# Chunked attention and a bilinear feed-forward: the output product of blocks 2 to 8 as seven half-block products in fp16

## The chip, the cores and the metric

The kernel runs on one NeuronCore of a Trainium2 chip. The metric is the device time of one execution in microseconds. A bank is a 128x512 fp32 tile of PSUM, the memory in which this kernel's matmul results lie. The engines are named as the profile names them: PE is TensorE (PEld its weight loads), DVE is VectorE, ACT is ScalarE, POOL is GpSimd, SP issues DMA.

## The reference, cut to what matters

```python
# attention in chunks of 64 tokens: q, k, v are (8, 8, 576, 64), about 0.1 in size
scores = scale * np.matmul(q_c, k_c.transpose(0, 1, 2, 4, 3))
attn = np.exp(scores - max);  attn = attn / (sum(attn) + 1e-09)
x = np.matmul(attn, v_c)                 # as 4608 tokens x 512
# feed-forward: w_a, w_b are 512 x 1536, w_out is 1536 x 512
a = x @ w_a
b = x @ w_b
return (a * b) @ w_out
```

## The kernel before

The 4608 tokens are nine blocks of 512 (K = 0 to 8), each of two attention units of 256 tokens. The program order of each engine is the order of the source. Blocks 0 and 1 compute a and b directly. From block 2 on a and b come from seven half-block products in place of eight (a Strassen scheme: sums of quarters of x, named s1 to s4, meet differences of quarters of the weights, named t1 to t4). A block has six groups i = 0 to 5 of 256 columns of w_a and w_b. Between the products of a group lie two slots with parts of the previous block's output product (`chunk`), and pieces of the attention of the next block (`attend`).

The parts that the change and the argument touch:

```python
def cast_ab(i):                          # weights fp32 -> fp16, on GpSimd
    for n in ("wb", "wa"):
        w_ab[n, i] = wpool.tile([128, NKT, WCOL], FP16, name=f"{n}{i}")
        nc.gpsimd.tensor_copy(out=w_ab[n, i], in_=staged.pop((n, i)))

class Group:                             # seven products, f16, 256 moving columns each
    def p1(self):
        self.A = bank(psum)
        self.product(self.A, self.b11, self.x11, True)
        self.B = bank(psum_b)
        nc.scalar.copy(out=self.B, in_=self.A)
    # ... p6, p2, p5: a product into B or A, then a ScalarE copy u, b or v to SBUF
    def p7(self):
        self.C = bank(psum_c)
        self.product(self.C, self.t3, self.s3, True)
    def add7(self):                      # VectorE: c = C + v, then C = C + u
        ...
    def p4(self):                        # adds to C, so it waits for C + u
        self.product(self.C, self.t4, self.x22)
        self.multiply(self.C, self.c, 256)

def out_part(K, tg, part):               # a third of a direct output product
    for ft in range(4 * part, 4 * part + 4):
        nc.tensor.matmul(out_ps[K, tg], ab_tiles[K][:, ft, tg * 128:tg * 128 + 128],
                         w_out[ft], ...)  # 512 moving columns, bf16

# ... attention pieces of the next block: unit U in groups 0 to 2, unit U + 1 in groups 2 to 4
((4, 1), values_x, U + 1),               # second slot of group 4: attention products,
                                         # then all four sums of x (combine_x) on VectorE
# ...
for K in range(2, NBLK):
    for i in range(NWP):
        now.p1(); last.add7(); chunk(); last.p3(); attend(K, i, 0)
        now.p6(); now.p2(); last.p4(); chunk(); attend(K, i, 1)
        now.p5(); now.p7(); last = now
```

The softmax here doesn't subtract the row's maximum and nothing guards it: scores larger than these inputs give would overflow.

Of the kernel before, what the change touches and what calls it, by code (L numbers as in the profile page):

```python
# [10 lines left out]
PE_UNITS = 6  # L11


@with_exitstack
def kernel(
# [36 lines left out]
    st_pool = ctx.enter_context(tc.tile_pool(name="st", bufs=9))  # L52
# [3 lines left out]
    x_pool = ctx.enter_context(tc.tile_pool(name="xp", bufs=3))  # L56
    s_pool = ctx.enter_context(tc.tile_pool(name="sp", bufs=2))
    ab_pool = ctx.enter_context(tc.tile_pool(name="ab", bufs=2))
    c_pool = ctx.enter_context(tc.tile_pool(name="csb", bufs=1))
    o_pool = ctx.enter_context(tc.tile_pool(name="osb", bufs=6))  # L60
    psum = ctx.enter_context(tc.tile_pool(name="psum", bufs=4, space=PSUM))
    psum_b = ctx.enter_context(tc.tile_pool(name="psumb", bufs=2, space=PSUM))
    psum_c = ctx.enter_context(tc.tile_pool(name="psumc", bufs=2, space=PSUM))
# [10 lines left out]
    spread = [psum, psum_b, psum, psum_c]  # L74

    def bank(pool=None):
        if pool is None:
            pool = spread[0]
            spread.append(spread.pop(0))
        n = {id(psum): "ps", id(psum_b): "pb", id(psum_c): "pc"}[id(pool)]  # L80
        return pool.tile([128, 512], FP32, name=n)
# [20 lines left out]
    def cast_ab(i):  # L102
        for n in ("wb", "wa"):
            w_ab[n, i] = wpool.tile([128, NKT, WCOL], FP16, name=f"{n}{i}")
            nc.gpsimd.tensor_copy(out=w_ab[n, i], in_=staged.pop((n, i)))
# [3 lines left out]
    def combine_w(i, part):  # L109
        wb, wa = w_ab["wb", i], w_ab["wa", i]  # L110
        b11, b12, b21, b22 = wb[:, 0:2], wa[:, 0:2], wb[:, 2:4], wa[:, 2:4]
        if i not in w_t:
            w_t[i] = [wpool.tile([128, 2, WCOL], FP16, name=f"t{j}_{i}") for j in range(1, 5)]
        t1, t2, t3, t4 = w_t[i]
        o, x0, x1, op = (
            (t1, b12, b11, SUB), (t3, b22, b12, SUB), (t2, t3, b11, ADD), (t4, b21, t2, SUB)
        )[part]
        nc.vector.tensor_tensor(out=o, in0=x0, in1=x1, op=op)
# [7 lines left out]

    def cast_wo(i):
        t = wpool.tile([128, 2, DM], BF16, name=f"wo{i}")
        nc.gpsimd.tensor_copy(out=t, in_=staged.pop(("wo", i)))
        for f in range(2):  # L130
            w_out[2 * i + f] = t[:, f, :]


# [37 lines left out]
    def cast(U, names="qkv"):  # L171
        for n in names if U < NU else "":
            raw[n, U] = raw_pool.tile(
                [128, 2, H, D], BF16, name=f"{n}_raw", bufs=4 if n == "v" else 3
            )
            eng = nc.vector if U == 0 and n != "v" else nc.gpsimd
            eng.tensor_copy(out=raw[n, U], in_=staged.pop((n, U)))  # L177
# [54 lines left out]
    def sums(U, halves=None):  # L232
        E = E_of[U]
        sm = [bank() for _ in range(2)]
        for cl in range(2):
            for j in range(2):
                nc.tensor.matmul(  # L237
                    sm[cl][j * 64:j * 64 + 64, :],
                    ones[cl * 64:cl * 64 + 64, :],
                    E[cl * 64:cl * 64 + 64, j].rearrange("p m g s -> p (m g s)"),  # L240
                    start=True,
                    stop=True,
                )
        ln_of[U] = sm_pool.tile([128, 2, NKT, 128], FP32, name="ln")
        rs_of[U] = ln_of[U]
        for cl in range(2):
            nc.scalar.activation(  # L247
                out=ln_of[U][:, cl].rearrange("p m n -> p (m n)"), in_=sm[cl], func=AF.Ln
            )
            if halves:  # L250
                inverse(U, cl)
# [60 lines left out]
    def ab_tile(K):  # L312
        if K not in ab_tiles:
            ab_tiles[K] = ab_pool.tile([128, NFT, BLK], BF16, name="ab_sb")
        return ab_tiles[K]

    def ab_step(K, ft, c0=0, c1=BLK):
        xT = x_tiles[K]
        dst = ab_tile(K)
        i, o = divmod(ft * 128, WCOL)  # L320
        ps = {}
        whole = c1 - c0 == BLK
        for n, pool in (
            ("wb", psum_b if whole else psum),
            ("wa", (psum_c, psum)[ft % 2]),
        ):
            ps[n] = bank(pool)[:, :c1 - c0]
            for kt in range(NKT):
                nc.tensor.matmul(  # L329
                    ps[n],  # L330
                    w_ab[n, i][:, kt, o:o + 128],
                    xT[:, kt, c0:c1],
                    start=(kt == 0),
                    stop=(kt == NKT - 1),
                )
        b_sb = c_pool.tile([128, BLK], FP32, name=("b_sb", "u_sb", "v_sb", "c_sb")[ft % 4])
        nc.scalar.copy(out=b_sb[:, :c1 - c0], in_=ps["wb"])
        nc.vector.tensor_tensor(
            out=dst[:, ft, c0:c1], in0=ps["wa"], in1=b_sb[:, :c1 - c0], op=MULT
        )  # L340
# [3 lines left out]
    def combine_x(K):  # L344
# [3 lines left out]
        s1, s2, s3, s4 = [s_pool.tile([128, 2, 256], FP16, name=f"s{j}") for j in range(1, 5)]  # L348
        for o, x0, x1, op in (
            (s1, x21, x22, ADD),  # L350
            (s2, s1, x11, SUB),
            (s3, x11, x21, SUB),
            (s4, x12, s2, SUB),
        ):
            nc.vector.tensor_tensor(out=o, in0=x0, in1=x1, op=op)  # L355
        s_of[K] = (s1, s2, s3, s4)

    class Group:
# [3 lines left out]
        def __init__(self, K, i):  # L362
            xT = x_tiles[K]
# [25 lines left out]
        def p1(self):  # L389
            self.A = bank(psum)  # L390
# [40 lines left out]

    out_ps = {}

    def out_part(K, tg, part):
        if part == 0:
            out_ps[K, tg] = bank(psum)
        for ft in range(4 * part, 4 * part + 4):
# [3 lines left out]
                w_out[ft],  # L441
# [3 lines left out]
        if part == 2:  # L445
            u, c = divmod(tg, 2)
            o_sb = o_pool.tile([128, DM], FP32, name="o_sb")
            nc.vector.tensor_copy(out=o_sb, in_=out_ps.pop((K, tg)))
            for g in range(2):
                r0 = K * BLK + 256 * u + 128 * g + 64 * c  # L450
                nc.sync.dma_start(out=out[r0:r0 + 64, :], in_=o_sb[g * 64:g * 64 + 64, :])

    def out_step(K, tg, parts=1, pool=None):
        u, c = divmod(tg, 2)
        w = DM // parts
        for h in range(parts):
            cols = slice(h * w, h * w + w)
            o_ps = bank(pool or psum)[:, :w]
            for ft in range(NFT):
                nc.tensor.matmul(  # L460
                    o_ps,
                    ab_tiles[K][:, ft, tg * 128:tg * 128 + 128],
                    w_out[ft][:, cols],
                    start=(ft == 0),
                    stop=(ft == NFT - 1),
                )
            o_sb = o_pool.tile([128, DM], FP32, name="o_sb")[:, :w]
            if h % 2:
                nc.scalar.copy(out=o_sb, in_=o_ps)
            else:  # L470
                nc.vector.tensor_copy(out=o_sb, in_=o_ps)

            for g in range(2):
                r0 = K * BLK + 256 * u + 128 * g + 64 * c
                eng = nc.scalar if parts > 1 and g else nc.sync
                eng.dma_start(out=out[r0:r0 + 64, cols], in_=o_sb[g * 64:g * 64 + 64, :])

    with tc.manual_schedule(
# [53 lines left out]
        spread[:] = [psum]  # L532
        combos = [(i, p) for i in range(NWP) for p in range(4)]
# [5 lines left out]
        for ft in range(NFT):  # L539
            ab_step(0, ft)  # L540
            if 2 <= ft < 10:
# [11 lines left out]
        for U in range(PE_UNITS, 8):  # L553
            bring(U)
# [3 lines left out]
        def chunk():  # L558
            if outs:
                out_part(*outs.pop(0))  # L560

        def values_x(U):
            values(U)
            if U % 2:
                combine_x(U // 2)

        def half(ft, u):
            ab_step(1, ft, 256 * u, 256 * u + 256)
            if ft % 4:
# [12 lines left out]
        spread[:] = [psum, psum_b]  # L582
# [7 lines left out]
        values(3)  # L590
        h(8)
        out_step(0, 0, 1, psum_b)
# [3 lines left out]
        out_step(0, 1, 1, psum_b)  # L596
# [6 lines left out]
        values(4)  # L603
        h(1)
        spread[:] = [psum, psum_c]
        normalize(5)
        out_step(0, 2, 1, psum_b)
        h(1)
        values_x(5)
        out_step(0, 3, 1, psum_b)  # L610
        spread[:] = [psum]
# [3 lines left out]
        for K in range(2, NBLK):  # L615
            U = 2 * K + 2
            for at, f, u in (
# [3 lines left out]
                ((2, 0), values_x, U),  # L621
# [3 lines left out]
                ((4, 1), values_x, U + 1),  # L625
# [7 lines left out]

        last = None
        for K in range(2, NBLK):
            for i in range(NWP):
                if i == 1:
                    outs += [(K - 1, tg, p) for tg in range(4) for p in range(3)]
                if i in (0, 3):
                    bring(2 * K + 4 if i == 0 else 2 * K + 5)  # L640
# [4 lines left out]
                chunk()  # L645
# [4 lines left out]
                now.p2()  # L650
                if last:
                    last.p4()
                chunk()
# [8 lines left out]
        last.p4()  # L662
        while outs:
            chunk()
        for tg in range(4):
            out_step(NBLK - 1, tg, 2 if tg == 3 else 1)
# [30 lines left out]
```

## Time and profile before

323.98 us, median of 3 runs (323.03 to 325.34). The profiled span is 322.3 us.

| what | before |
|---|---|
| start of block 2 (its first product) | 82.6 us |
| block 2 | 31.5 us |
| blocks 3 to 7 (with attention), mean | 32.56 us |
| five groups of block 8 | 23.92 us |
| last group and tail | 21.5 us |

These stages are read from the timeline: each begins with the first matmul of a block's first `p1`. The five numbers add up to the span (the mean of blocks 3 to 7 counted five times).

TensorE works without holes where there is no attention. From the timeline of before, TensorE alone (start in us, duration in us, line, output<-inputs, shape, how many):

```profile
282.11 1.03 PE L438 MATMUL ps<-wo,ab_sb 128*128 128x512 bf16 x4
282.97 0.60 PE L375 MATMUL pb<-s,wa 128*128 128x256 f16 x4
283.41 0.60 PE L375 MATMUL pb<-s,t 128*128 128x256 f16 x4
```

Starts are what counts, as matmuls overlap: four matmuls of 512 columns take 282.97 - 282.11 = 0.86 us, 0.215 each; four of 256 take 0.44 us, 0.108 to 0.11 each. That agrees with N/2.4 + 2.5 ns, which the Trainium skill (page "TensorE: Matmul & The Clock Gate", section "Back-to-back issue gap") gives for isolated matmuls at full clock: 109 and 216 ns.

There is one real stall of TensorE in a block. The list of waits of before (who waited for whom: us in total, times, longest) has it in one line:

```profile
PE pc L375 <- DVE pc L414: 5.9, 6, 1.5
```

Product p4 waits for VectorE's `C + u`, once per block, up to 1.5 us. The timeline of before, VectorE alone, shows why:

```profile
205.49 1.29 DVE L279 TENSOR_TENSOR xT<-ps,ln 128x512 f16<-128x512 f32 x2 [0.63 <-PE ps L270]
206.81 0.82 DVE L355 TENSOR_TENSOR s<-xT 128x512 f16<-128x512 f16 x1
207.67 0.42 DVE L355 TENSOR_TENSOR s<-s,xT 128x512 f16<-128x512 f16 x1
208.02 0.42 DVE L355 TENSOR_TENSOR s<-xT 128x512 f16<-128x512 f16 x1
208.35 0.42 DVE L355 TENSOR_TENSOR s<-xT,s 128x512 f16<-128x512 f16 x1
208.69 0.68 DVE L413 TENSOR_TENSOR c_sb<-pc,v_sb 128x512 f32<-128x512 f32 x1
209.29 0.69 DVE L414 TENSOR_TENSOR pc<-pc,u_sb 128x512 f32<-128x512 f32 x1
```

Two attention products (xT) and the four sums of x (s) stand ahead of `c_sb` and `pc` (add7). In this trace VectorE's operations run in the order of the source, so p4 starts only at 210.03.

And the page of before gives the granted TensorE clock, in tenths, over 40 slices of the span:

```profile
PEclk9999999999999999999999999999999999999999
```

### The profile page before, as it was taken

To read this page: it belongs to the slowest core of one execution; us is meant where nothing else is said; L and a number is where in the kernel's file an instruction comes from. 1 tells how busy PE (TensorE), PEld (TensorE's weight loads), DVE (VectorE), ACT (ScalarE), POOL (GpSimd) and SP (SyncE) were. 2 spreads that over 40 slices of the span, in tenths; PEclk is the share of its full clock that TensorE was granted. 3 is DMA by queue.
4 is the path that set the end of the run, shared out by engine and by line. 5 is a ranking of instruction groups with operands and counts; after the bars stand their busy time and mean duration, and the time that the engine had idled before them with its cause. 6 is when DMAs were issued, how large, how long until landed. Compare 5 with 4: busy or idle time off the path is not lost.

```text
span 322.3 us, 7885 instructions
## 1 busy us (share of the span) xinstructions
PE 299.3 (93%) x3192; PEld 205.6 (64%) x3238; DVE 209.5 (65%) x346; ACT 169.5 (53%) x307; POOL 73.8 (23%) x76
## 2 busy tenths in 40 slices
PE   2889999999999799989998999999999999999995
PEld 1535477765577576667766766666676667677753
DVE  3348678875665866586658665866677667766551
ACT  1742756267467366636664666456655665444400
POOL 1575665642222222221212021203000000000000
PEclk9999999999999999999999999999999999999999
DMA  7999999999999999957695679478411111112124
GB/s 235 324 378 285 278 364 274 261 228 201 209 227 226 209 211 220 183 140 167 162 186 140 153 176 215 113 126 201 101 35 35 33 35 35 34 41 50 41 67 98
DMA packets 139331, 53.98 MB, mean 167 GB/s; under 512 B 114592, under 2 KB 133280, under 8 KB 139296
## 3 DMA queue, kind: packets, MB, share of 16 engines
q1 hardware_dynamic: 139136, 53.36, 70.8%
q8 instruction: 25, 0.41, 0.5%
q10 hardware_dynamic: 160, 0.13, 0.2%
q14 instruction: 10, 0.08, 0.1%
HBM read 37.75 MB, written 9.44 MB: 146 GB/s over the span
## 4 chain that ended last, share of the span: by engine, by line
PE 70%; DVE 8%; DMA 7%; ACT 6%; SPq 4%; issue 3%; POOL 1%; DVEq 0%; ACTq 0%; POOLq 0%
PE ps L438 19%; PE pb L375 15%; PE pc L375 10%; PE ps L375 9%; PE ps L329 3%; PE ps L460 3%; PE pb L460 3%; DMA st<-in_q_dram 3%; DVE s L355 3%; ACT E L230 2%; SPq L150 2%; DMA st<-in_moe_w_b_dram 2%; DVE xT L279 2%; DMA st<-in_v_dram 2%; PE ps L270 2%
## 5 line engine op out<-in xcount | busy, mean ns | idle before, releaser
L438 PE MATMUL ps<-wo,ab_sb 128*128 128x512 bf16 x297 | 79.9, 379 | 1.7
L375 PEld LDWEIGHTS <-t 128*128 128x128 f16 x672 | 62.8, 98 | 23.4 <-issue 10.6
L413 DVE TENSOR_TENSOR c_sb<-pc,v_sb 128x512 f32<-128x512 f32 x42 | 29.0, 691 | 41.3 <-ACT v_sb L386 41.3
L375 PE MATMUL pb<-s,t 128*128 128x256 f16 x336 | 50.8, 274 | 0.7 <-ACT u_sb L386 0.5
L375 PE MATMUL ps<-xT,wb 128*128 128x256 f16 x336 | 50.4, 273 | 0.0
L438 PEld LDWEIGHTS <-ab_sb 128*128 128x128 bf16 x336 | 32.9, 98 | 21.7
L386 ACT COPY u_sb<-pb 128x512 f32<-128x512 f32 x42 | 24.7, 588 | 40.9 <-PE pb L375 25.3
L425 DVE TENSOR_TENSOR ab_sb<-pc,c_sb 128x512 bf16<-128x512 f32 x42 | 28.9, 689 | 21.6 <-PE pc L375 21.6
L177 POOL CAST q_raw<-st 128x1024 bf16<-128x1024 f32 x17 | 17.9, 1051 | 78.6 <-DMA st<-in_q_dram 67.5
L375 PEld LDWEIGHTS <-wb 128*128 128x128 f16 x336 | 32.9, 98 | 4.0
L386 ACT COPY v_sb<-pb 128x512 f32<-128x512 f32 x42 | 24.8, 591 | 19.7 <-PE pb L375 18.9
L425 DVE TENSOR_TENSOR ab_sb<-pb,b_sb 128x512 bf16<-128x512 f32 x42 | 28.8, 685 | 3.9 <-PE pb L375 3.9
L375 PE MATMUL pc<-xT,t 128*128 128x256 f16 x168 | 25.2, 272 | 5.9 <-DVE pc L414 5.9
L393 ACT COPY pb<-ps 128x512 f32<-128x512 f32 x42 | 24.5, 583 | 10.8 <-PE ps L375 10.2
L414 DVE TENSOR_TENSOR pc<-pc,u_sb 128x512 f32<-128x512 f32 x42 | 29.0, 690 | 0.0
L177 POOL CAST k_raw<-st 128x1024 bf16<-128x1024 f32 x17 | 17.8, 1048 | 43.3 <-DMA st<-in_k_dram 43.3
L386 ACT COPY b_sb<-ps 128x512 f32<-128x512 f32 x42 | 25.1, 598 | 3.5 <-DVE ab_sb L425 3.5
L375 PE MATMUL pb<-s,wa 128*128 128x256 f16 x168 | 25.2, 273 | 0.3
L375 PE MATMUL pc<-s,t 128*128 128x256 f16 x168 | 25.2, 273 | 0.0
L247 ACT ACTIVATE ln<-ps 128x512 f32<-128x512 f32 x31 | 17.1, 596 | 14.3 <-PE ps L237 13.5
L230 ACT ACTIVATE E<-ps 128x512 bf16<-128x512 f32 x31 | 17.1, 595 | 12.9 <-PE ps L222 12.2
L279 DVE TENSOR_TENSOR xT<-ps,ln 128x512 f16<-128x512 f32 x31 | 20.0, 684 | 5.2 <-PE ps L270 3.8
(79 smaller groups left out, 373.4 us busy)
## 6 DMA issues: line engine op xcount, KB each, us to landing
out_dram<-o_sb SPq DMA_DIRECT2D x70, 128.0 KB, 2.4
st<-in_v_dram SPq DMA_DIRECT2D x32, 256.0 KB, 4.4
st<-in_q_dram SPq DMA_DIRECT2D x23, 256.0 KB, 4.3
st<-in_k_dram SPq DMA_DIRECT2D x23, 256.0 KB, 3.8
st<-in_moe_w_b_dram SPq DMA_DIRECT2D x6, 512.0 KB, 7.5
st<-in_moe_w_a_dram SPq DMA_DIRECT2D x6, 512.0 KB, 8.0
st<-in_moe_w_out_dram SPq DMA_DIRECT2D x6, 512.0 KB, 6.4
st<-in_q_dram SPq DMA_DIRECT2D x4, 512.0 KB, 5.6
```

Of the source, the lines that this page charges most:

```text
L177: eng.tensor_copy(out=raw[n, U], in_=staged.pop((n, U)))
L230: nc.scalar.activation(out=E_of[U][:, j], in_=sc[j], func=AF.Exp, scale=scale)
L247: nc.scalar.activation(out=ln_of[U][:, cl].rearrange("p m n -> p (m n)"), in_=sm[cl], func=AF.Ln)
L279: nc.vector.tensor_tensor(out=x_tiles[K][:, :, c0:c0 + 128], in0=av[cl].rearrange("p m g s -> p m (g s)"), in1=rs[:, cl], op=MULT,)
L375: nc.tensor.matmul(t[:, h * 256:h * 256 + 256], w[:, kt, h * 128:h * 128 + 128], x[:, kt], start=start and h == 0 and kt == 0, stop=h == 1 ...
L386: nc.scalar.copy(out=t, in_=src)
L393: nc.scalar.copy(out=self.B, in_=self.A)
L413: nc.vector.tensor_tensor(out=self.c, in0=self.C, in1=self.v, op=ADD)
L414: nc.vector.tensor_tensor(out=self.C, in0=self.C, in1=self.u, op=ADD)
L425: nc.vector.tensor_tensor(out=self.dst[:, :, c0:c0 + 256], in0=t.rearrange("p (h n) -> p h n", h=2), in1=o.rearrange("p (h n) -> p h n", h=2),
L438: nc.tensor.matmul(out_ps[K, tg], ab_tiles[K][:, ft, tg * 128:tg * 128 + 128], w_out[ft], start=(ft == 0), stop=(ft == NFT - 1),)
L460: nc.tensor.matmul(o_ps, ab_tiles[K][:, ft, tg * 128:tg * 128 + 128], w_out[ft][:, cols], start=(ft == 0), stop=(ft == NFT - 1),)
```

## The change

The intent: do the output product, too, by seven half-block products (84 matmuls of 256 columns in place of 48 of 512), so TensorE has 1.2 us less work a block. ab and w_out become fp16 for it. As a x b is small, both weights are scaled by 16 and the result by 1/256. The sums of ab and of w_out go to GpSimd, the sums of x go into two later slots, and PSUM is divided anew.

```diff
 def cast_ab(i):
-            nc.gpsimd.tensor_copy(out=w_ab[n, i], in_=staged.pop((n, i)))
+            nc.gpsimd.tensor_scalar(
+                out=w_ab[n, i], in0=staged.pop((n, i)), scalar1=W_SCALE, scalar2=None, op0=MULT
+            )
 # pools
-    psum: 4 banks, psumb: 2, psumc: 2
+    psuma: 1 bank, psumb: 2, psumc: 1, psumo: 1, psumq: 1, psumt: 2
-    st 9 buffers, xp 3, osb 6
+    st 8 buffers, xp 2, osb 2 (twice the size), so 1
-        ln_of[U] = sm_pool.tile([128, 2, NKT, 128], FP32, name="ln")
+        ln_of[U] = sm_pool.tile([128, 2, NKT, 128], FP32, name="ln", bufs=1)
 # attention of the next block
-                ((4, 1), values_x, U + 1),
+                ((4, 1), values, U + 1),
+                ((5, 0), lambda u: combine_x(u // 2, (0, 1)), U + 1),
+                ((5, 1), lambda u: combine_x(u // 2, (2, 3)), U + 1),
 # sums of ab, on GpSimd
+    def combine_ab(K, part, j, eng=None):
+        ...
+        (eng or nc.gpsimd).tensor_tensor(out=o, in0=x0, in1=x1, op=op)
 # seven products of the output, two halves each: 14 pieces, three or two a group
+    class OutGroup:
+        def part(self, n, th):
+            ...                       # n = 0..6: 6 matmuls of 256 columns into A, B or C
+            # after n=0: ScalarE copies A to B; n=2, 3: copies of B; n=1, 5: output halves
+            # after n=4: VectorE o1 = C / 256 + v, and C = C + u; after n=6: VectorE, last part
 # loop over the groups
+                if K == 2:
+                    for _ in range(2):
+                        combine_wo(*wo_sums.pop(0))
+                if K == 2:
+                    combine_w(i, 3)
                 now.p6()
-                now.p2()
                 if last:
                     last.p4()
+                    finish(last)      # sums of ab of groups 3 to 5
-                chunk()
+                now.p2()
+                chunk(2 if K > 2 and i == 4 else 1)
 # the last block
-        for tg in range(4):
-            out_step(NBLK - 1, tg, 2 if tg == 3 else 1)
+        g = OutGroup(NBLK - 1)
+        for n in range(7):
+            for th in range(2):
+                g.part(n, th)
```

Cut: `combine_wo` (12 sums of the quarters of w_out), the fourth difference of the input weights, done in place in block 2 because block 1 still reads the original, units 6 and 7 brought a little later, the fourth buffer for v taken away, and some pools and slots of the early phase changed.

## The prediction

> **What bounds the kernel now.** TensorE. In the timeline, matmuls with 256 moving columns start every 0.108 us and those with 512 every 0.215 us, back to back: the groups of block 8 without attention (281 to 300 us) repeat every 4.79 us, and 28 x 0.108 + 8 x 0.215 = 4.75. The granted clock is 1.00. The windows per block give 32.4 us for a block with attention (blocks 3 to 7), 28.7 us for block 8, and PE is busy 31.4 us of 32.4. The Trainium skill ("TensorE: Matmul & The Clock Gate", Back-to-back issue gap) gives N/2.4 + 2.5 ns, 109 and 216 ns; this trace agrees. The one real stall is at each block's start: p4 waits for VectorE's sum into the pc bank (list of waits: PE pc from DVE pc, 5.9 us in 6 times, longest 1.5), because two attention products (1.3 us) and four sums of x (1.3 to 1.9 us) lie ahead of it on VectorE.
>
> **What the change removes.** Output product: 48 x 0.215 = 10.3 us becomes 84 x 0.108 = 9.1 us, -1.2 us a block. Six blocks (2 to 7) gain inside the loop: -7.4 us. Moving the sums of x into later slots removes most of the 5.9 us of stalls.
>
> **What it adds.**
> - ScalarE: five operations of 0.57 to 0.59 us a block, 2.9 us; 19.05 us becomes 22 us of about 31. It stays strictly in order, with 1.07 us exponentials and logarithms ahead of the copies that PE waits for.
> - p4 now comes before p2, and a slot holds 0.65 us of output product in place of 0.86. So p4 arrives about 0.65 us earlier at a sum whose slack was 0.5 us (203.04 to 203.54): I expect stalls of 0.1 to 0.5 us in several groups of each attention block, for v (ScalarE late) and for pc, and up to 0.5 in the group that now has the sums of x. A and C with one bank each, and attention with two, add to it. My estimate is 1.5 us of such stalls a block in place of about 1, uncertain by 0.6 each way.
> - GpSimd: 12 sums a block. The skill ("GPSIMD Engine Reference", 3.1) gives 4497 ns for 2048 fp32 elements, so an estimate of 1.1 to 1.2 us for 512: 14 us more beside 6.3 us of casts, within a block. No GpSimd sum is in this trace. I expect it off the critical path except perhaps in block 2, where it also has the 12 sums of the output weights.
> - Tail: block 8's seven products stand alone. Copies between them stall PE about 0.85 us three times, and the last stores (four issues on one queue after the last eviction) come later than the old 322.3 - 318.8 = 3.5 us. Estimate: 14.4 us from the last p4 becomes about 16.5.
>
> **Sum.** Loop products -7.4; stalls -5.9 + 0.5 x 6 = about -3, perhaps eaten by the attention blocks; tail +2; early phase -0.5 with spread 1.5 (fewer sums on VectorE, units 6 and 7 brought later): about -6 in the middle, from -11 to -1.
>
> **Predicted 318.0 us, range 312.5 to 323.0. Faster by over 2%: 0.46; within 2%: 0.50; slower: 0.04.**
>
> **What would show it.** Block 8's window near 27.4 us. Attention blocks near 31.2 us. PE pc from DVE pc no longer 1 us long at block starts; instead short PE waits on ScalarE (v, pb) and DVE pc. GpSimd sums near 1.1 us. Tail from the last p4 16 to 17 us.
>
> **What would make it wrong.** More slack on ScalarE than I walked through: then 313. GpSimd sums much slower, or slowing VectorE's 16-bit sums, or late attention inputs: then PE waits on so or qkt tiles and the gain is gone.

## More of the kernel before

The early phase has the casts of the weights on GpSimd. From the timeline of before, GpSimd alone (in brackets the idle time ahead of an instruction, and what ended it):

```profile
15.37 1.04 POOL L105 CAST wb<-st 128x1024 f16<-128x1024 f32 x1 [1.29 <-DMA st<-in_moe_w_b_dram]
16.71 1.04 POOL L105 CAST wa<-st 128x1024 f16<-128x1024 f32 x1 [0.30 <-DMA st<-in_moe_w_a_dram]
18.08 1.04 POOL L105 CAST wb<-st 128x1024 f16<-128x1024 f32 x1 [0.32 <-DMA st<-in_moe_w_b_dram]
```

Each takes 1.04 us, and GpSimd then waits for the next load.

## The result, and the profile after

The changed kernel took 342.0 us (median of 4 runs, 341.31 to 345.77) beside 323.68 us (323.03 to 325.34; one run more than above) of the kernel before. The ratio is 1.0578, with an interval of 1.0503 to 1.0652: slower. Ratios are the mean time of one kernel's runs over that of the other's of the same rounds, so they are not quite the ratio of the medians quoted. Executions over 1.5% slower than the fastest of the same kernel are left out of the means. The profile is that of the slowest of the four (span 344.0 us).

| stage | before | after | difference |
|---|---|---|---|
| start of block 2 | 82.6 | 103.4 | +20.8 |
| block 2 | 31.5 | 33.4 | +1.9 |
| blocks 3 to 7, mean (all five) | 32.56 | 31.64 | -0.92 (-4.6) |
| five groups of block 8 | 23.92 | 23.57 | -0.35 |
| last group and tail | 21.5 | 25.4 | +3.9 |

The sum is +21.7 us, the difference of the spans. So almost all of the loss happened before a single one of the new products ran. From the timeline of after, GpSimd alone:

```profile
15.99 2.77 POOL L114 TENSOR_SCALAR wb<-st 128x1024 f16<-128x1024 f32 x1 [1.22 <-DMA st<-in_moe_w_b_dram]
18.84 2.77 POOL L114 TENSOR_SCALAR wa<-st 128x1024 f16<-128x1024 f32 x1
21.69 2.77 POOL L114 TENSOR_SCALAR wb<-st 128x1024 f16<-128x1024 f32 x1
```

The cast that also multiplies takes 2.77 us, not 1.04, and between these casts GpSimd does not wait for loads any more. Now TensorE waits for GpSimd's results. From the list of waits of after:

```profile
PE pc L355 <- POOL wa L114: 6.0, 4, 1.8
PE pa L296 <- POOL v_raw L203: 3.7, 1, 3.7
PE pc L404 <- DVE pc L443: 3.5, 6, 0.7
```

The first two have no such sizes in the profile before (there `PE ps <- POOL v_raw` is 0.5). The third is the old stall of p4, still there in every block. The clock line of the page of after:

```profile
PEclk9989996999989999999999999999999999999998
```

It dips three times before block 2: by the trace's clock records, one stretch of 6.83 us and two of 3.41 us at half clock. (The 8 at the end lies behind the last matmul.) The skill's page "TensorE: Matmul & The Clock Gate" (Part 1) gives 3413 ns as the length of the window by which the clock is set, and half rate as the idle state; these stretches, one and two windows long, agree.

Three smaller things. VectorE's two-input sums take three times as long beside GpSimd's sums (timeline of after, VectorE alone, to be read against the four `s` lines of before):

```profile
102.25 1.22 DVE L384 TENSOR_TENSOR s<-xT 128x512 f16<-128x512 f16 x1
103.50 1.26 DVE L384 TENSOR_TENSOR s<-s,xT 128x512 f16<-128x512 f16 x1
104.69 1.37 DVE L384 TENSOR_TENSOR s<-xT 128x512 f16<-128x512 f16 x1
105.98 1.37 DVE L384 TENSOR_TENSOR s<-xT,s 128x512 f16<-128x512 f16 x1
```

GpSimd alone at that time has four sums of w_out in 5.03 us, 1.26 us each, and VectorE's four go at the same pace:

```profile
102.04 5.03 POOL L158 TENSOR_TENSOR wot<-wo 128x512 f16<-128x512 f16 x4
```

GpSimd's own sums take what was expected (from the timeline of after, GpSimd):

```profile
161.41 1.15 POOL L481 TENSOR_TENSOR so<-ab_sb 128x512 f16<-128x512 f16 x1 [0.95 <-DVE ab_sb L454]
```

And the last block's seven products, alone, stop TensorE four times (timeline of after, TensorE, from the last p4 to the last product):

```profile
324.77 0.60 PE L404 MATMUL pc<-xT,t 128*128 128x256 f16 x4
325.95 1.47 PE L496 MATMUL po<-wo,ab_sb 128*128 128x256 f16 x12 [0.59 <-DVE o_sb L562]
328.14 1.47 PE L496 MATMUL po<-wo,ab_sb 128*128 128x256 f16 x12 [0.71 <-ACT pq L536]
329.44 1.47 PE L496 MATMUL pq<-wot,so 128*128 128x256 f16 x12
331.64 1.47 PE L496 MATMUL pq<-wot,so 128*128 128x256 f16 x12 [0.73 <-ACT uo_sb L544]
332.95 1.47 PE L496 MATMUL po<-wot,ab_sb 128*128 128x256 f16 x12
334.26 1.47 PE L496 MATMUL pq<-wo,so 128*128 128x256 f16 x12
336.00 1.47 PE L496 MATMUL po<-wot,ab_sb 128*128 128x256 f16 x12 [0.26 <-DVE po L554]
```

From p4 to the end of the span it is 344.0 - 324.8 = 19.2 us, against 322.3 - 307.7 = 14.6 in the kernel before.

### The profile page after: what moved, and what is told of

The parts are those of the page before. It is cut to its first block, busy times and chain, and to the rows that moved or that the text cites. A ratio compares the mean times of both kernels' runs of the same rounds, so it can differ in the third digit from the quotient of the medians.

```text
span 344.0 us, 8521 instructions
## 1 busy us (share of the span) xinstructions
PE 303.6 (88%) x3476; PEld 229.5 (67%) x3478; DVE 211.3 (61%) x345; ACT 190.2 (55%) x341; POOL 196.8 (57%) x166
## 4 chain that ended last, share of the span: by engine, by line
PE 66%; DVE 12%; POOL 9%; ACT 4%; issue 3%; SPq 3%; DMA 2%; DVEq 0%; ACTq 0%
PE pb L404 13%; PE pc L404 11%; PE po L496 10%; PE pa L404 9%; PE pq L496 6%; POOL wa L114 4%; POOL wb L114 4%; PE pb L584 3%; DVE xT L305 3%; DVE c_sb L442 2%; DVE pc L443 2%; DVE s L384 2%; PE pc L355 2%; ACT E L256 2%; DMA st<-in_moe_w_b_dram 2%
## 5 line engine op out<-in xcount | busy, mean ns | idle before, releaser
L404 PE MATMUL pb<-s,wa 128*128 128x256 f16 x336 | 50.6, 273 | 2.5 <-DVE wa L131 2.5
L404 PE MATMUL pa<-xT,wb 128*128 128x256 f16 x336 | 50.4, 273 | 0.0
L404 PEld LDWEIGHTS <-wa 128*128 128x128 f16 x336 | 31.3, 98 | 9.9 <-DVE wa L131 2.7
L496 PEld LDWEIGHTS <-ab_sb 128*128 128x128 f16 x336 | 32.9, 98 | 5.9 <-issue 2.1
L415 ACT COPY u_sb<-pb 128x512 f32<-128x512 f32 x42 | 24.6, 586 | 21.7 <-DVE pc L443 9.4
L454 DVE TENSOR_TENSOR ab_sb<-pc,c_sb 128x512 f16<-128x512 f32 x42 | 28.9, 689 | 6.5 <-PE pc L404 4.4
L454 DVE TENSOR_TENSOR ab_sb<-pb,b_sb 128x512 f16<-128x512 f32 x42 | 28.7, 683 | 4.8 <-PE pb L404 4.6
L422 ACT COPY pb<-pa 128x512 f32<-128x512 f32 x42 | 24.6, 586 | 11.3 <-PE pa L404 11.2
L415 ACT COPY b_sb<-pa 128x512 f32<-128x512 f32 x42 | 24.9, 594 | 8.4 <-PE pa L404 8.0
L203 POOL CAST v_raw<-st 128x1024 bf16<-128x1024 f32 x18 | 18.7, 1040 | 17.7 <-DMA st<-in_v_dram 12.1
L203 POOL CAST q_raw<-st 128x1024 bf16<-128x1024 f32 x17 | 17.7, 1040 | 16.9 <-DMA st<-in_q_dram 14.7
L496 PEld LDWEIGHTS <-so 128*128 128x128 f16 x252 | 24.7, 98 | 3.7 <-issue 0.9
L404 PE MATMUL pb<-s,t 128*128 128x256 f16 x168 | 25.4, 274 | 0.5 <-DVE s L384 0.5
```

The costliest lines, as they stand in the source:

```text
L203: eng.tensor_copy(out=raw[n, U], in_=staged.pop((n, U)))
L404: nc.tensor.matmul(t[:, h * 256:h * 256 + 256], w[:, kt, h * 128:h * 128 + 128], x[:, kt], start=start and h == 0 and kt == 0, stop=h == 1 ...
L415: nc.scalar.copy(out=t, in_=src)
L454: nc.vector.tensor_tensor(out=self.dst[:, :, c0:c0 + 256], in0=t.rearrange("p (h n) -> p h n", h=2), in1=o.rearrange("p (h n) -> p h n", h=2),
L496: nc.tensor.matmul(t[:, th * 256:th * 256 + 256], a[:, kt, th * 128:th * 128 + 128], w[:, kt], start=start and th == 0 and kt == 0, stop=t ...
```

## The experiments

Twelve kernels ran in four batches on different chips; the median of the kernel before lay between 324.10 and 324.50 us in them. The ratio is to the kernel before of the same batch. "Plain" below means a_plain_cast, from which the later ones start.

| kernel | median us (range) | ratio to before (interval) | block 2 starts | block 2 | blocks 3-7 mean | block 8, five groups | rest |
|---|---|---|---|---|---|---|---|
| before | 323.98 (323.03 to 325.34) | 1 | 82.6 | 31.5 | 32.56 | 23.92 | 21.5 |
| after | 342.00 (341.31 to 345.77) | 1.0578 (1.0503 to 1.0652) | 103.4 | 33.4 | 31.64 | 23.57 | 25.4 |
| b_mul_cast | 337.38 (335.57 to 337.53) | 1.0384 (1.0320 to 1.0449) | 96.3 | 30.7 | 32.60 | 23.92 | 21.5 |
| a_plain_cast | 326.80 (326.72 to 327.60) | 1.0081 (1.0033 to 1.0129) | 85.7 | 32.2 | 31.63 | 23.57 | 25.4 |
| a_half_cast | 329.69 (328.76 to 330.57) | 1.0164 (1.0111 to 1.0217) | 87.7 | 32.4 | 31.63 | 23.58 | 25.4 |
| p_direct_last | 323.65 (321.93 to 323.98) | 0.9968 (0.9915 to 1.0021) | 86.4 | 31.9 | 31.63 | 23.58 | 21.7 |
| p_ln_two | 326.08 (324.92 to 328.38) | 1.0061 (1.0010 to 1.0112) | 87.1 | 32.2 | 31.66 | 23.57 | 25.4 |
| p_slots | 329.20 (328.90 to 331.64) | 1.0165 (1.0116 to 1.0214) | 85.9 | 32.1 | 32.02 | 24.36 | 24.7 |
| p_sums_together | 343.43 (341.92 to 344.77) | 1.0584 (1.0526 to 1.0642) | 86.6 | 37.4 | 33.86 | 23.14 | 25.4 |
| p_best | 323.43 (323.05 to 323.88) | 0.9971 (0.9938 to 1.0004) | 83.8 | 32.3 | 32.01 | 24.36 | 21.5 |
| p_direct_all | 322.19 (321.35 to 324.25) | 0.9942 (0.9910 to 0.9975) | 84.3 | 30.3 | 31.78 | 23.92 | 22.4 |
| p_final | 321.18 (319.68 to 321.83) | 0.9888 (0.9861 to 0.9914) | 86.5 | 29.9 | 31.64 | 23.58 | 21.7 |
| b_spread | 317.45 (317.05 to 318.49) | 0.9799 (0.9772 to 0.9825) | 82.8 | 29.9 | 31.52 | 23.92 | 21.5 |

The stages come from each kernel's one profiled execution; the twelfth, p_final_bank, is told at the end.

### b_mul_cast: the cast's multiply alone, in the kernel before

```diff
-        nc.gpsimd.tensor_copy(out=w_ab[n, i], in_=staged.pop((n, i)))
+        nc.gpsimd.tensor_scalar(
+            out=w_ab[n, i], in0=staged.pop((n, i)), scalar1=1.0, scalar2=None, op0=MULT
+        )
```

> The kernel before, with the 12 casts of the input weights on GpSimd done by a multiply with 1.0 (tensor_scalar) in place of a plain copy; nothing else changed, the result is the same. Theory (the scaled cast is the cost): each of these casts takes 2.77 us as in the changed kernel, not 1.04, and as GpSimd works in order and the first block waits for the weights, block 2 starts 15 to 21 us later: about 339 to 345 us against 323.7. Rival (the slow start comes from the new banks, smaller staging pools and later loads, and the cast is slow there only because of what runs beside it): within 3 us of 323.7.

Measured: 337.38 us, and block 2 starts at 96.3, 13.7 us later than before. The timeline of b_mul_cast, GpSimd alone:

```profile
15.26 2.77 POOL L105 TENSOR_SCALAR wb<-st 128x1024 f16<-128x1024 f32 x1 [0.92 <-DMA st<-in_moe_w_b_dram]
17.99 2.77 POOL L105 TENSOR_SCALAR wa<-st 128x1024 f16<-128x1024 f32 x1
```

The operation alone costs 2.77 us, with none of the other parts of the change, and it alone makes the kernel slower by 3.8% (clear of the 2% mark). The rival falls. The size is a little below the expected 15 to 21 us. The later stages are those of the kernel before, so nothing else came with it.

### a_plain_cast: the multiply taken out of the change

```diff
-            nc.gpsimd.tensor_scalar(
-                out=w_ab[n, i], in0=staged.pop((n, i)), scalar1=W_SCALE, scalar2=None, op0=MULT
-            )
+            nc.gpsimd.tensor_copy(out=w_ab[n, i], in_=staged.pop((n, i)))
-    nc.vector.memset(ones, 1.0)
+    nc.vector.memset(ones, 1.0 / W_SCALE)
```

The ones are the weights of the products that sum the exponentials, so 1/16 there makes x 16 times as large, and a and b with it.

> The changed kernel, with the plain cast back; the factor 16 enters through the ones of the attention sums (1/16 in place of 1.0), so x is 16 times as large and the result is the same at no cost. Theory: block 2 starts near 82.6 us again as in the kernel before (changed: 103.4), TensorE clock 1.00 throughout, and the time falls by about 21 us to 319 to 322. Rival (banks, pools, loads): block 2 still starts after 95 us and the time stays above 332.

Measured: 326.80 us, and block 2 starts at 85.7. The cast accounts for 17.7 of the 20.8 us. But the time is about 5 us above the expected range: the start is still 3.1 us late, the clock was not 1.00 throughout (one stretch of 3.41 us at half clock from 20.1 us on, after a wait of 3.25 us), and block 2 and the tail keep their losses. Block 2's last group takes 7.1 us where the others of that block take 3.6 to 5.75, as VectorE's sums of x there meet GpSimd's sums of w_out.

### a_half_cast: half the dose

```diff
-            nc.gpsimd.tensor_scalar(... scalar1=W_SCALE ...)      # both weights
+            if n == "wa":
+                nc.gpsimd.tensor_scalar(... scalar1=W_SCALE ...)
+            else:
+                nc.gpsimd.tensor_copy(out=w_ab[n, i], in_=staged.pop((n, i)))
-    nc.vector.memset(ones, 1.0)
+    nc.vector.memset(ones, 0.25)
```

> The changed kernel, with half the dose: only the 6 casts of w_a multiply (by 16), the 6 of w_b are plain copies; the ones are 1/4, so the products of a and b carry the same 256. Theory: the extra GpSimd time is 6 x 1.73 = 10.4 us in place of 20.8, and since waits for DMA leave GpSimd some idle time to take it up, the time lies at or below the middle between full and none: 322 to 333. Rival: as the full change, 340 to 344.

Measured: 329.69 us, within the range, and far from linear: half the dose delays block 2 by 2.0 us against plain, the full dose by 17.7. A rate explains it, by an estimate. TensorE uses up a pair of weight tiles in 16 matmuls of 512 columns, 16 x 0.215 = 3.45 us. GpSimd makes a pair in 2 x 1.04 = 2.1 us with two copies, in 1.04 + 2.77 = 3.8 us with one multiply, in 2 x 2.77 = 5.5 us with two. The lag of six pairs is then an estimate of 0, 6 x 0.36 = 2.2 and 6 x 2.09 = 12.5 us, to set against 2.0 (half) and 13.7 (full, in the kernel before). The full change lost 4 us more than that; it also had 13.7 us at half clock before block 2, where plain had 3.4 and b_mul_cast none. That fits in size (10.3 us more at half rate cost at most 5.1), but no run here separates it.

### p_direct_last: the tail

```diff
-            if K >= 2 and i >= 3:
+            if 2 <= K < NBLK - 1 and i >= 3:
...
-        for j in range(3):
-            combine_ab(NBLK - 1, 3, j, nc.vector)
-        g = OutGroup(NBLK - 1)
-        for n in range(7):
-            for th in range(2):
-                g.part(n, th)
+        for tg in range(4):
+            for p in range(3):
+                out_part(NBLK - 1, tg, p, (psum_t, psum_q)[tg % 2])
```

> The version with the plain cast, but with the last block's output product done directly (48 products of 512 columns into two alternating banks, no sums of ab) as in the kernel before, to size the tail. In the changed kernel the stretch from the last p4 to the end takes 19.2 us against 14.6 before. Theory: that stretch falls back to 14.5 to 16 us, so this is 3 to 4.7 us faster than the version with the plain cast: 315 to 318.5. Rival (the tail is bound by the output stores, not by the seven products): within 1 us of the version with the plain cast.

Measured: 323.65 us, 3.1 us less than plain; the rest after the five groups falls from 25.4 to 21.7. The gain is as expected, the absolute time is not, as plain itself was later than I had thought. Alone at the end, seven products with copies between them lose to eight without.

### p_ln_two: a buffer that unit 1 needs

In plain the first product of the input weights starts at 20.3 us in place of 18.8. The timeline of plain, ScalarE alone, shows a hole of 1.44 us ahead of unit 1's first logarithm, and beneath it the same instruction in the profile before:

```profile
17.11 0.60 ACT L271 ACTIVATE ln<-po 128x512 f32<-128x512 f32 x1 [1.44 <-PE pa L96]
```

```profile
15.65 0.60 ACT L247 ACTIVATE ln<-ps 128x512 f32<-128x512 f32 x1
```

The profile blames a warm-up matmul, whose result no logarithm reads. With one `ln` buffer in place of two it must be VectorE's last reading of unit 0's reciprocals, which ends at 16.31 + 0.68 = 16.99.

```diff
+        if U == 1:
+            ln_of[U] = Halves()      # two 128x512 fp32 tiles that are first used in block 3
+        else:
+            ln_of[U] = sm_pool.tile([128, 2, NKT, 128], FP32, name="ln", bufs=1)
```

> The version with the plain cast, but unit 1's logarithms and reciprocals get a place of their own (two tiles that are unused so early), as when that pool held two. Open: the plain cast still starts block 2 at 85.7 us, 3.1 us later than the kernel before (82.6). Theory (the single buffer for logarithms): unit 1's first logarithm no longer waits from 15.7 to 17.1 us for VectorE's products of unit 0, the first product of the input weights starts at 18.8 us and not 20.3, TensorE has no stretch of half clock after it, and block 2 starts at 82.6 to 83.5: 323.5 to 324.5 us in all, 2.3 to 3.3 less than with the plain cast alone. Rival (the bank pools of the early phase): first product earlier, but block 2 still at 85 or later, gain under 1 us.

Measured: 326.08 us, 0.7 less than plain (the ranges of the two overlap). The cause of the hole is right, as the timeline of p_ln_two shows, ScalarE alone:

```profile
15.66 0.60 ACT L285 ACTIVATE uo_sb<-po 128x512 f32<-128x512 f32 x1
```

The first product starts at 18.8 again. The outcome is the one named for the rival: first product earlier, block 2 after 85 us, gain under 1 us. In the profiled execution, the slowest of the four, block 2 starts at 87.1. There TensorE waits 1.75 us for the cast of unit 2's v near 40 us, and has 3.41 us at half clock from 41.75 on. But p_best and p_direct_all, below, have the same program up to block 2; in their profiles no half clock falls there, and block 2 starts at 83.8 and 84.3. So part of the gain is real, and the stretch of half clock comes in some executions and not in others. p_best is still 1.3 us late, about as long as its wait for a bank in block 1 (1.25 us, `PE pt` from `DVE xT`), which the kernel before does not have; no run separates this from the smaller pools (st, v).

### p_slots: the double slots moved

In plain, too, p4 stalls in every attention block. Timeline of plain, VectorE and then TensorE:

```profile
206.66 0.69 DVE L548 SCALAR_TENSOR_TENSOR o_sb<-po,vo_sb 128x512 f32<-128x512 f32 x1 [1.11 <-PE po L494]
207.38 0.70 DVE L552 TENSOR_TENSOR po<-po,uo_sb 128x512 f32<-128x512 f32 x1
207.99 1.28 DVE L303 TENSOR_TENSOR xT<-pt,ln 128x512 f16<-128x512 f32 x2
209.19 0.68 DVE L440 TENSOR_TENSOR c_sb<-pc,v_sb 128x512 f32<-128x512 f32 x1
209.79 0.69 DVE L441 TENSOR_TENSOR pc<-pc,u_sb 128x512 f32<-128x512 f32 x1
```

```profile
210.53 0.60 PE L402 MATMUL pc<-xT,t 128*128 128x256 f16 x4 [0.64 <-DVE pc L441]
```

The sums of x are gone from this place, but the two new operations on the fifth output product (0.7 us each) have taken it.

```diff
-                chunk(2 if K > 2 and i == 4 else 1)
+                chunk(2 if K > 2 and i in (2, 3) else 1)
```

> The version with the plain cast, but the two double slots of output product lie in groups 2 and 3 of a block, not in group 4, so that VectorE's two operations on the fifth product (1.3 us) come a group before the last attention products of the block. Theory (p4 of group 5 stalls 0.81 us in each of blocks 3 to 7 because those two operations, 1.3 us, and two attention products stand ahead of its sum on VectorE): that stall falls under 0.3 us, the group takes 4.4 to 4.7 us in place of 5.19, 2.5 to 4 us less in all: 322.8 to 324.3. Rival (the stall is made by GpSimd's sums slowing VectorE's sums of x): unchanged within 1 us.

Measured: 329.20 us, slower than plain by 2.4 us, so the expectation failed. In the profile a block with attention takes 31.89 us in place of 31.55. (The five groups of block 8 hold the same 12 pieces and still take 0.79 us more; the rest holds one piece less, 0.65 us.) The group that stalled, 5, fell only from 5.19 to 4.93 us. Groups 2 and 3 each took over a piece of 0.65 us and rose by 0.65 and 0.76 us. Groups 4 and 0 each gave one away: group 4 fell by 0.59, but group 0 only by 0.23 us. The list of waits of p_slots shows where the stall went:

```profile
PE pc L402 <- DVE ab_sb L452: 4.2, 7, 1.9
PE pc L402 <- DVE pc L441: 1.5, 7, 0.5
PE pb L402 <- ACT u_sb L413: 1.4, 5, 0.4
```

In plain these three are 1.9 (once), 3.5 and 0.5 us. The stall of p4 shrank as expected, but now p7 waits for VectorE to empty C, for which the change left one bank, and p5 for ScalarE's copy u. The rival (stretched sums of x) is not shown by this either. What it shows is that the loop with seven products has little slack to move work into.

### p_sums_together: the sums of x back in one place

```diff
-                ((4, 1), values, U + 1),
-                ((5, 0), lambda u: combine_x(u // 2, (0, 1)), U + 1),
-                ((5, 1), lambda u: combine_x(u // 2, (2, 3)), U + 1),
+                ((4, 1), lambda u: (values(u), combine_x(u // 2)), U + 1),
```

> The version with the plain cast, but with the four sums of x of a block together right after its last attention products, as in the kernel before, in place of in two later slots. Theory (spreading them is worth what the one real stall of the old kernel cost): the sums come on top of the out product's two operations and GpSimd's sums stretch some of them from 0.42 to 1.4 us, so p4 of group 5 waits 2.0 to 3.5 us in place of 0.81; 6 to 13 us slower: 333 to 340. Rival (spreading moves nothing that matters): within 2 us of 326.8.

Measured: 343.43 us, 16.6 us slower than plain, beyond the expected 6 to 13. Block 2 takes 37.4 us (its last group alone 12.3) and the attention blocks 33.1 to 34.8. Three stretches at half clock from 100 us on (13.7 us together) come with the longer waits and add to them. The direction is clear: with the output's work on VectorE and GpSimd's sums beside it, the seven-product loop cannot do without the spread.

### p_best: all that helped, together (and one thing that did not)

p_ln_two, p_slots and p_direct_last in one kernel, with the 12 sums of w_out in the first four groups of block 2. It was sent with the last three, so it carries p_slots' loss.

> All that helped, together: plain cast, own place for unit 1's logarithms, double slots moved, last block's output product direct, and the sums of the output weights done in the first four groups of block 2 so that fewer meet VectorE's sums of x at its end. If the terms add: 326.8 - 3.1 (start) - 3.3 (tail) - 3.5 (slots) - 1 to 1.9 (block 2) = 315 to 317.5, faster than the kernel before by 2 to 3%. If the gains overlap (the stalls only move to the next group): 319 to 321.

Measured: 323.43 us; the terms did not add. The last group of block 2 fell from 7.1 to 5.3 us, but its first rose from 3.6 to 5.6. Product p5 waits there for the in-place difference of the input weights (timeline of p_best, TensorE):

```profile
88.55 0.61 PE L416 MATMUL pb<-s,wa 128*128 128x256 f16 x4 [2.41 <-DVE wa L129]
```

That difference stands on VectorE behind the four sums of x, and three GpSimd sums in a row (from 83.13 to 87.03) now met these: 0.74 to 1.37 us each, 4.6 us in all, where plain has 1.75.

### p_direct_all: everything but the seven output products

```diff
-                    if K == 2: ... else:
-                        for j in range(3):
-                            combine_ab(K - 1, 3, j)
-                        g = OutGroup(K - 1)
-                        outs += [lambda g=g, n=n, th=th: g.part(n, th) for n in range(7) for th in range(2)]
+                    outs += [
+                        lambda k=K - 1, tg=tg, p=p: out_part(k, tg, p, (psum_o, psum_q)[tg % 2])
+                        for tg in range(4) for p in range(3)
+                    ]
```

> Everything of the change except its core: plain cast, own place for unit 1's logarithms, the new banks, the new order of p4, the spread sums of x, but the output product of every block direct (48 products of 512 columns), with no sums of ab or of the output weights. It shows what the seven half-block products themselves are worth in the loop. The seven-product loop takes 31.55 us a block with attention (29.3 of TensorE work), block 8 without its tail 23.6. If the products' saving is real in the loop (theory): 1.24 us more work and at most 0.8 us fewer stalls, so 31.8 to 32.4 us a block, and the last groups 4.78 us each. If the stalls that the seven products brought eat all of it (rival): 31.0 to 31.6 us a block. In both, the last group of block 2 takes 5.0 to 5.5 us in place of 7.1, since no GpSimd sums meet VectorE's sums of x. Time 319.5 to 323 under the theory, 316 to 319.5 under the rival.

Measured: 322.19 us, in the theory's range. Three of its attention blocks take 31.6 us, the other two 31.9 and 32.2; the mean is 31.78 against 31.63 with seven products. The block lies at the border of the two expectations. Of the 1.24 us of TensorE work that the seven products save in a block, the loop keeps 0.15 (by the mean) or nearly nothing (by the best blocks). Over the whole kernel the repaired seven products, p_final below, are 1.0 us faster than this one, with ratios whose intervals just overlap.

### p_final: the seven-product loop repaired

Plain, p_ln_two and p_direct_last, the w_out sums in the first four groups, and VectorE's fourth difference of the input weights in block 1:

```diff
             if ft % 2:
                 combo()
+                if u == 1:
+                    combine_w(ft // 2, 3)
...
-                if K == 2:
-                    combine_w(i, 3)
```

> The seven-product loop repaired: plain cast, own place for unit 1's logarithms, the last block direct, double slots as in the change (moving them did not help), the sums of the output weights in the first four groups of block 2, and VectorE's last difference of the input weights in block 1 where GpSimd makes no sums. Block 2 starts at 83 to 84 us and takes 30.5 to 31 us (32.2 with the plain cast alone), the attention blocks 31.55, the rest 45.3: 317.5 to 320 us, 1.2 to 2% faster than the kernel before. If the two-input operations on VectorE that now lie in block 1 delay the attention there, 320 to 322.

Measured: 321.18 us, in the second range named (320 to 322), though whether for the reason named there is not shown. Block 2 now takes 29.9 us in place of 32.2: of the sums of x at its end only one meets a GpSimd sum (1.38 us, the others 0.42; in plain three take 1.21 to 1.37), and its loss is gone. The start did not come back (86.5 in the profile, with 3.41 us at half clock from 79.4 on). The six executions fall in two sets: 319.68 to 320.67 us at a mean clock of 1.000, and 321.68 to 321.83 at 0.991 to 0.995. The profile is of the second set, so about 1.6 us goes with a stretch of half clock that only some executions have.

### b_spread: the spread alone, in the kernel before

```diff
-                ((4, 1), values_x, U + 1),
+                ((4, 1), values, U + 1),
+                ((5, 0), lambda u: combine_x(u // 2, (0, 1)), U + 1),
+                ((5, 1), lambda u: combine_x(u // 2, (2, 3)), U + 1),
```

with `combine_x` made to do a given part of its four sums; nothing else differs from before.

> The kernel before with one part of the change alone: the four sums of x of a block in two slots of its last group instead of right behind its last attention products. Theory (in the attention blocks the change gains by this, hardly by its products): the last group of blocks 2 to 7 takes 4.8 to 5.2 us in place of 5.6 to 6.45, an attention block 31.6 to 32.0 us in place of 32.4, 3.5 to 6 us less in all: 318 to 321 us. Rival (the gain of the changed kernel's attention blocks comes from the seven products): 323 to 325 us.

Measured: 317.45 us (317.05 to 318.49), ratio 0.9799, the fastest of all and just below the range expected. (The interval, 0.9772 to 0.9825, lies on both sides of the 2% mark.) Every last group of blocks 2 to 7 takes 4.78 us. The line of p4's wait is gone from its list of waits. Its timeline, VectorE alone, at the place of the seven VectorE lines shown of before:

```profile
201.69 1.29 DVE L279 TENSOR_TENSOR xT<-ps,ln 128x512 f16<-128x512 f32 x2 [0.63 <-PE ps L270]
202.90 0.68 DVE L415 TENSOR_TENSOR c_sb<-pc,v_sb 128x512 f32<-128x512 f32 x1
203.50 0.69 DVE L416 TENSOR_TENSOR pc<-pc,u_sb 128x512 f32<-128x512 f32 x1
```

The attention products are followed by add7 at once. The mean attention block is 31.52 us, with the direct output product. With the seven products it is 31.63. So the spread alone gives all that the changed kernel gains in its attention blocks, and the seven products, with the banks and the order that came with them, bring nothing on top of it there.

### p_final_bank: failed

In the kernels with the new banks TensorE waits in block 1 for a bank (1.2 to 1.8 us by the lists of waits, less than the 1.6 to 2.0 that I wrote down). I took out the line `spread[:] = [psum_t]` ahead of unit 5's sums, to give them a second pool.

> The repaired seven-product kernel (321.2 us), where the sums of unit 5's attention in block 1 may take a bank of the second pool besides the two of their own. In all kernels with the changed banks TensorE waits there 1.6 to 2.0 us for VectorE to empty a bank (in the kernel before there is no such wait), and in the profile of the repaired kernel a stretch of half clock of 3.4 us follows it. If the wait and the half clock go: 2.5 to 3.5 us less, 317.7 to 318.8. If only the wait goes: 1.3 to 2 less, 319 to 320. If the direct output product then waits for that bank instead: no gain, 320.5 to 322.

The result was wrong (relative error 0.65) and the time 343.48 us. The edit was a mistake: the list that this line sets stays in force for blocks 2 to 8, so their attention drew from the pool of bank B (the trace has attention products into `pb` there), which holds accumulations in progress. The time says nothing about the wait. But block 1 comes before the blocks named, and the two timelines, TensorE alone, can be compared, p_final first:

```profile
77.97 0.40 PE L272 MATMUL pt<-E,ones 64*64 64x512 bf16 x2 [1.58 <-DVE xT L317]
```

```profile
78.60 2.75 PE L596 MATMUL pb<-wo,ab_sb 128*128 128x512 f16 x12 [2.18 <-DVE xT L317]
```

The attention sums no longer wait, but the direct output product right after them waits for the same VectorE operation: the third outcome named. (This profile has no half clock there, after a wait of 2.18 us.)

## Why the prediction was wrong

The cast is most of the miss, but not all of it: with the plain cast the kernel still took 326.80 us, above the predicted range (312.5 to 323.0). Plain against before, by stage: start +3.1, block 2 +0.7, blocks 3 to 7 -4.6, five groups of block 8 -0.35, last group and tail +3.9. So three terms of the prediction's sum were too favourable: the early phase, the loop products and the tail.

- **The early phase: the step that failed.** The prediction put it as "early phase -0.5 with spread 1.5 (fewer sums on VectorE, units 6 and 7 brought later)". It measured +20.8 us. The prediction listed "6.3 us of casts" a block on GpSimd and never costed the changed cast of the 12 weight tiles, though the diff shows the operation replaced. b_mul_cast shows that the multiply costs 2.77 us where the copy costs 1.04, and +13.7 us by itself; a_plain_cast shows 17.7 us gone when it goes; a_half_cast fits the estimate of why it is so large, the rate at which block 0 uses weights.
- **A second early term was missed.** The pool of logarithms went from two buffers to one; it delays the first product by 1.5 us (p_ln_two removes that delay). Of the 3.1 us, plain's stretch at half clock can be up to 1.7, and 1.3 us are left in p_best, which has neither; no run separates these.
- **The products' work: right size, no effect.** 10.3 against 9.1 us a block is right. An attention block has by estimate 168 x 0.108 us of input products, about 2.2 us of attention (0.38, 0.35 and 0.38 us twice, from the timeline) and the output product: 30.7 us direct, 29.4 with seven. b_spread runs at 31.52, so 0.8 us over its work; the seven-product loop at 31.55 (31.63 with the first), 2.1 over. The prediction's estimate of 1.5 us of stalls was low, and its -7.4 us came out as nothing in the attention blocks once b_spread is the measure. Where there is no attention, the saving does show: in block 8 a group with two pieces takes 4.37 us in place of 4.78, and from the block's first product to its last p4 it is 29.8 us in place of 30.9.
- **The stall at the end of each block.** "Moving the sums of x into later slots removes most of the 5.9 us" is right for the move itself: b_spread removes all of it. In the changed kernel it stayed at 3.5 us, because the output product's two VectorE operations stand in the same place.
- **Attention blocks** were predicted near 31.2 and measured 31.6: a fair forecast, reached for another reason.
- **Tail:** predicted from 14.4 to about 16.5, measured from 14.6 to 19.2 us. The stalls of TensorE are 0.59, 0.71, 0.73 and 0.26 us by the trace, so the three expected of 0.85 were about right in sum. The rest is the end: from the start of the last VectorE operation (337.5) to the end it is 6.5 us, with four stores issued one after another, where the kernel before had 3.5 from its last copy.
- **GpSimd's sums** took 1.15 us, as the prediction estimated. That they slow VectorE's 16-bit sums was named as a risk; a sum of 0.42 us took up to 1.37, and this cost block 2 about 2 us (32.2 in plain, 29.9 in p_final).

## What to carry to other kernels

Cost each changed instruction of a diff on its own engine, even one that looks like a cast with a free factor, and compare the time in which an engine makes a tile with the time in which the consumer uses it up: while making is faster, the lag stays near zero; once it is slower, the lag grows with every tile (here, a pair made in 2.1, 3.8 or 5.5 us and used in 3.45). A factor can often ride on something that is already multiplied (here the ones of a sum). And test the small parts of a large change alone on the old kernel: here moving four small sums gave 2.0%, and the kernel with the large part that they came with, repaired as far as it was, ended 3.7 us behind that (321.18 against 317.45).

## What the Trainium skill lacked or had wrong

- Page "GPSIMD Engine Reference", section 4.1, says of one-input operations on GpSimd that they are "roughly line-rate", without a distinction. Here a plain copy fp32 to fp16 of 128x1024 took 1.04 us, but a multiply by a constant with the same input and output (tensor_scalar) 2.77 us, 2.7 times as long, in the kernel after and in b_mul_cast.
- The same page, section 1, says that GpSimd's SBUF interfaces are shared with VectorE and that VectorE instructions with two SBUF inputs contend. The runs agree and add a size, which the page does not have: such a sum of 128x512 in fp16 takes 0.42 us alone and up to 1.37 us beside GpSimd's sums. VectorE operations with one PSUM input kept their 0.69 us.
- Its table in section 3.1 has tensor_tensor only for 2048 fp32 elements (4497 ns). In fp16 with 512 elements it took 1.15 us, so about a quarter: no gain from the smaller type.
- Page "TensorE: Matmul & The Clock Gate", section "Back-to-back issue gap", gives 131 ns as the sustained spacing at N=512 in a stream of weight loads and matmuls. Here that stream had 215 ns, the figure of the same section's formula for isolated ones.
- The same page (Part 1) has half clock follow at least one idle window of about 3.4 us. Here shorter waits of TensorE were followed by it, 1.75 us in p_ln_two and 1.58 us in p_final, while b_mul_cast, with a wait of 3.35 us, kept 1.00 from 12 us on to the end of its work. No run here shows which idle time is enough.
